# The passage from the long convolution into the MLP: copies and turns in halves, two tiles normalised on VectorE, ten fillers, and a new list order

## Chip, core and metric

One core of a Trainium2 chip runs the whole program. TensorE (PE in the rows; PEld is its weight load) multiplies, VectorE (DVE), ScalarE (ACT) and GpSimd (POOL) work on elements, SyncE (SP) issues most transfers. The metric is the device time of one execution in microseconds, the median of three runs. The profile is one more execution, read on its own clock: 0 is the start of the span.

## The reference, cut to what matters

An adaptive-LayerNorm block on 2048 rows of 640 columns in bf16. First half: normalise, scale and shift by a modulation, then a gated long convolution over the rows (a length-4096 Fourier product, done here as matrix products), times q, added to x. Second half: normalise again, scale and shift, then a gated MLP (gMLP) whose gate mixes rows by a 2048 x 2048 matrix.

```python
h = _layernorm(x, axis=-1) * (1 + ca) + sa
x = x + ga * _A_ref(h, A_k, A_v, A_shift_k, A_ssm_k, A_ssm_D)     # y = irfft(rfft(kv) * rfft(ssm_k)), q * y
h = _layernorm(x, axis=-1) * (1 + cb) + sb
z = _gelu(einsum('bsd,df->bsf', h, w_in))                         # 864 columns z1, 864 columns z2
g = einsum('ts,bsf->btf', w_sp, _layernorm(z2)) + b_sp
x = x + gb * einsum('bsf,fd->bsd', z1 * g, w_out)
```

The second normalisation needs all 640 columns of a row, so the MLP can begin only when the last 128 columns of the convolution are done. That place is the passage.

## The kernel before

The convolution runs in five units u = 0 to 4 of 128 columns. Per unit there are eight stages st: a forward product into `pu` (matrices M), a product with the filter's spectrum on VectorE (`prod`, L495: `Tf` or `T`), in half the stages a sum on GpSimd or VectorE (`csum`, L509: `W`), an inverse product into `pz` (matrices G) and a copy `zc` of 128 x 512 into `Z`, on ScalarE (L278, helper `copy`). Then the rows have to be turned: units 0 to 3 by a DMA transpose of `Z` into `ZT` and products `y` with `Ebd` (`y_mult`, VectorE multiply `ym` at L770), unit 4 on TensorE (`last_stage_pe`): four blocks of eight 128 x 128 transposes (`zfl`, L831) into `pu`/`pz`, four copies `zk` of 128 x 1024 into two `X` buffers, then products `yl` of 128 x 16 for each of four row groups g (512 rows each), a multiplication `yml` (L856), the addition to x `res` (L808) and statistics `ln2` (L814).

`norm_piece` and `flip_piece` make the MLP's input of group 0 in two pieces of two row tiles n: `ag2` gathers statistics (L943), GpSimd makes 1/sqrt in two instructions (`rstd_from_var`, L218 and L219), VectorE makes `nmr2` (L947), any of three engines normalises (`zx`, L957/L959/L961), TensorE transposes (`hfl`, L972), VectorE and ScalarE scale and shift (`hmod`, L985/L983). `z_group` then multiplies: a `zz` is five matmuls of 128 x 432 into `pu`/`pz`, sixteen `zz` a group, 64 in all, each followed by a gelu on ScalarE (L1034). Groups 1 to 3 are turned by a DMA transpose from SyncE (L1003) and scaled by five `hmod2` (L1011/L1009). After that come the mixing products (L1126) and the projections (L1335, L1348).

What sets the order: `Plan.op` records every piece of work with the engines that may run it and what it reads and writes; the string `ORDER` lists engine and number of each, and `run` emits them in that order. Each engine works through its own list strictly in order, waiting where an operand is not there yet. Buffers come from `SLOTS`. `FILLS` gives the matmuls (128 x 512, `ident` times `ident`) in each of the `fill` entries, whose result nothing reads; in this kernel three of them run near the start and one stands ahead of the first `zz`.

Of the kernel before, what the change touches and what calls it, by code (L numbers as in the profile page):

```python
# [15 lines left out]
P = 128  # L16
# [8 lines left out]
NU = 5  # L25
# [12 lines left out]
FILLS = (4, 2, 2, 2, )  # L38
# [9 lines left out]
G5 D18 A1 S83 G0 G110 S2 P7 S23 G109 G6 D13 A4 D14 G25 A16 D15 D111 P1041 D10 S26 D112 P8 A38 D17 D113 A11 G89 D130  # L48
A115 D136 P1044 S24 P153 S84 S91 A154 P156 P39 D131 P41 A158 A133 A132 S27 P1043 G90 D118 G134 D40 A137 D119 S3 A114
P45 A155 A157 D124 P159 D125 S531 D135 P162 G96 A121 A120 D42 A160 G122 P43 D19 S532 A161 A127 G116 P235 D46 A163 G117  # L50
A126 A164 D44 D128 P141 G129 D20 P85 P179 A21 G22 A236 P173 D142 G143 A180 D86 A174 P241 P9 A242 D535 G123 S28 D29 P87
P181 D88 P184 D183 A182 P239 A186 P167 P177 S30 G47 A12 P147 D539 A168 P165 A178 A240 A166 D536 A537 P144 D148 S31 P175
A176 G139 D540 D145 P237 P187 A185 A541 D189 P48 P54 S534 P171 D188 D49 D55 P190 A172 D192 P50 P52 D51 A191 G56 D53
P193 P219 P92 P150 S573 A238 S97 A538 D194 P225 S533 D93 D220 G32 G146 G195 P57 G149 G196 A151 P94 P169 D226 G152 P259
A542 A170 P203 P209 D58 A260 P61 P197 G65 D95 A550 P265 D204 D221 D62 G205 P574 D210 P229 G222 D230 G206 A198 G102 D543
A266 P59 P223 P261 A551 P247 S576 P213 D60 A575 A262 P207 A248 P63 S33 A224 D214 P199 A552 D200 P263 D546 P227 A264
P249 G544 A250 P243 A244 D64 P577 G74 D34 P309 G231 D578 G215 A208 A310 P98 P255 A256 P257 P211 P267 D545 S579 D547
G557 G232 P311 G216 A258 S35 D99 D548 A553 G561 A228 D268 A312 P100 D549 P66 D101 P251 P277 A252 D554 A212 P233 D278
A234 P313 P245 P201 D269 P580 A314 G558 G562 D67 D581 P315 S103 G270 G555 D556 P253 A202 A246 P283 P271 A316 P591 D559
# [98 lines left out]
def kernel(  # L158
# [80 lines left out]
    with ExitStack() as pctx:  # L239
# [578 lines left out]
        def last_stage_pe(u):  # L818
# [3 lines left out]
            for b, qb in enumerate(range(0, NQ, QB)):  # L822
# [640 lines left out]
```

## Time and profile before

| | |
|---|---|
| runs (us) | 305.56, 306.22, 306.85, median 306.22 |
| span of the profiled execution | 303.8 us |
| TensorE busy | 293.1 us (96%) |
| VectorE, GpSimd, ScalarE busy | 86%, 61%, 54% |
| TensorE's granted clock | full, but for a stretch from 127 to 133.8 us |

No time but the span is known for the profiled execution. The runs' median is 2.4 us above it; what lies around the span is taken as unchanged. Busy time of TensorE is close to the span, but pipelined matmuls count as busy also while they are spaced widely, so the passage has to be read in time order.

### The profile page before, as it was taken

The numbers are of one execution on the slowest core, as the hardware profiler recorded it, in microseconds if no ns is written. First come the engines' busy times: TensorE is split into PE (matmuls) and PEld (weight loads), VectorE is DVE, ScalarE is ACT, GpSimd is POOL, SyncE is SP. The second block draws the span as 40 slices with busy tenths as digits, with TensorE's granted clock in tenths as the row PEclk, the third lists the DMA queues.
The fourth block names the chain that finished last, engine by engine and source line by source line (L and its number), as shares of the span: only waits on it lengthen the run. The fifth ranks groups of instructions, "written<-read, shape, count | busy, mean of one in ns | idle before, by whom it ended". The sixth has DMA issues, their size and how long they took to land.

```text
span 303.8 us, 7152 instructions
## 1 busy us (share of the span) xinstructions
PE 293.1 (96%) x2827; PEld 207.0 (68%) x2827; DVE 260.4 (86%) x527; ACT 164.0 (54%) x299; POOL 186.8 (61%) x213
## 2 busy tenths in 40 slices
PE   6899999999999999799999999999999999999996
PEld 2788999999989988645555555555555555665664
DVE  8899999999989999989595988988678798886794
ACT  5989999998888865446665779500111102111110
POOL 5463788839769997577537342099531863476771
PEclk9999999999999999869999999999999999999999
DMA  7999869792397978005997900057654446452433
GB/s 143 270 242 271 194 177 282 134 223 39 77 186 163 287 122 276 2 2 105 157 234 154 197 0 4 0 117 150 132 133 90 102 112 141 102 84 73 91 83 121
DMA packets 117155, 41.57 MB, mean 137 GB/s; under 512 B 102557, under 2 KB 117122, under 8 KB 117122
## 3 DMA queue, kind: packets, MB, share of 16 engines
q1 hardware_dynamic: 116968, 41.08, 62.0%
q8 instruction: 22, 0.36, 0.5%
q14 instruction: 11, 0.09, 0.1%
q10 hardware_dynamic: 154, 0.05, 0.1%
HBM read 16.60 MB, written 2.63 MB: 63 GB/s over the span
## 4 chain that ended last, share of the span: by engine, by line
PE 80%; DVE 8%; SPq 5%; DMA 3%; issue 2%; POOL 1%; ACT 0%; DVEq 0%; POOLq 0%
PE ps L1126 23%; PE pu L275 19%; PE pz L275 17%; PE po L1335 5%; PE sm L275 5%; PE s L275 4%; SPq L570 3%; DVE Tf L495 3%; PE po L1348 3%; DMA ZT<-in_A_v_dram 3%; PE pz L1126 2%; PE pu L1126 1%; DVE Z L616 1%; SPq L585 1%; DVE ot L1394 1%
## 5 line engine op out<-in xcount | busy, mean ns | idle before, releaser
L275 PEld LDWEIGHTS <-Z 128*128 128x128 bf16 x320 | 32.0, 100 | 28.8 <-issue 3.0
L275 PE MATMUL pu<-X,M 128*128 128x128 bf16 (+1 forms) x480 | 45.6, 237 | 0.9 <-DVE Tf L495 0.7
L509 POOL TENSOR_TENSOR W<-Tf 128x256 bf16<-128x256 f32 x42 | 30.7, 745 | 15.0 <-DVE Tf L495 9.0
L275 PEld LDWEIGHTS <-M 128*128 128x128 bf16 x480 | 36.7, 98 | 4.2 <-issue 1.6
L1126 PEld LDWEIGHTS <-S 128*128 128x128 bf16 x256 | 25.0, 98 | 20.8
L275 PE MATMUL pu<-big,Z 128*128 128x432 bf16 x160 | 34.6, 360 | 0.0
L278 ACT CAST X<-s 128x1024 bf16<-128x1024 f32 x32 | 32.7, 1021 | 3.3 <-PE s L275 3.2
L275 PE MATMUL pz<-big,Z 128*128 128x432 bf16 x160 | 33.0, 349 | 0.0
L495 DVE TENSOR_TENSOR Tf<-pu,KH 128x1024 f32<-128x1024 f32 x25 | 30.3, 1215 | 1.2 <-ACT Z L278 0.5
L1132 ACT COPY m<-ps 128x432 f32<-128x432 f32 x7 | 3.6, 521 | 49.8 <-PE ps L1126 41.0
L1126 PEld LDWEIGHTS <-wT 128*128 128x128 bf16 x192 | 18.8, 98 | 15.3
L278 ACT CAST Z<-pz 128x512 bf16<-128x512 f32 x40 | 23.5, 596 | 4.9 <-PE pz L275 4.7
L275 PEld LDWEIGHTS <-G 128*128 128x128 bf16 x330 | 24.6, 98 | 1.8 <-issue 0.4
L278 ACT CAST KH<-pu 128x512 bf16<-128x512 f32 x40 | 23.1, 592 | 3.8 <-PE pu L275 3.4
L1126 PE MATMUL ps<-X,wT 128*128 128x432 bf16 x112 | 22.7, 346 | 0.0
L1126 PE MATMUL ps<-X,S 128*128 128x432 bf16 x112 | 22.6, 346 | 0.0
L1040 DVE BATCH_NORM_STATS2 stz<-X 128x6 f32<-128x432 bf16 x32 | 18.1, 588 | 5.0 <-ACT X L1034 4.9
L1126 PE MATMUL ps<-T,S 128*128 128x432 bf16 x112 | 22.2, 346 | 0.0
L275 PE MATMUL sm<-dg,big 128*128 128x128 bf16 x320 | 20.7, 219 | 1.1 <-DVE Z L616 1.0
L275 PEld LDWEIGHTS <-big 128*128 128x128 bf16 x320 | 18.9, 98 | 2.0 <-issue 1.6
L495 DVE TENSOR_TENSOR T<-pu,KH 128x1024 bf16<-128x1024 f32 x15 | 18.2, 1215 | 1.9 <-PE pu L275 1.8
L275 PEld LDWEIGHTS <-X 128*128 128x128 bf16 x288 | 17.8, 98 | 2.2 <-POOL X L433 0.7
(223 smaller groups left out, 666.7 us busy)
## 6 DMA issues: line engine op xcount, KB each, us to landing
wm<-in_w_mod_dram SPq DMA_DIRECT2D x6, 800.0 KB, 4.9
xt<-in_A_q_dram SPq DMA_DIRECT2D x4, 640.0 KB, 5.6
out_dram<-ot SPq DMA_DIRECT2D x15, 160.0 KB, 1.9
big<-in_B_w_in_dram SPq DMA_DIRECT2D x2, 1080.0 KB, 7.8
X<-in_A_ssm_k_dram SPq DMA_DIRECT2D x4, 512.0 KB, 6.2
ZT<-in_A_v_dram SPq DMA_DIRECT2D x1, 1024.0 KB, 7.6
big<-in_A_v_dram SPq DMA_DIRECT2D x1, 1024.0 KB, 7.8
w_o<-in_B_w_out_dram SPq DMA_DIRECT2D x6, 160.0 KB, 3.5
```

Source lines behind the costliest of these rows:

```text
L275: nc.tensor.matmul(o, lhsT=w, rhs=x, start=start, stop=stop)
L278: (e.copy if e is nc.scalar else e.tensor_copy)(dst, src)
L495: e.tensor_tensor(T_[:], (tl[pu] if src is None else tl[src])[:, :, :, None, :].to_broadcast(shape), tl[KH][:, :, None, :, :].to_broadcast ...
L509: e.tensor_tensor(tl[W][:, :, o, :], T_[:, :, 0, o, :], T_[:, :, 1, 1 - o, :], op=ALU.add if o else ALU.subtract)
L570: e.dma_start_transpose(k_of(u)[:, KPAD + h * m:KPAD + (h + 1) * m], A_k[0, h * m:(h + 1) * m, u * DU:(u + 1) * DU])
L585: e.dma_start(v_of(0, ns.start, NT // n) if u0 == 0 else tl[name][:], v_nat[:, ns, ds])
L616: e.tensor_tensor(dst, tl[ps][:].rearrange("p n (c g) -> p n c g", g=8), v_of(u, i * SCH, SCH).rearrange("p n (c g) -> p n c g", g=8), op= ...
L1040: op("D", "stz", lambda e, i=i, n=n, fc=fc: e.bn_stats(out=stz[:, n, fc, :], in_=tl[z2][:, i, fc * FC:(fc + 1) * FC]), r=[(z2, (i, fc))], ...
L1126: nc.tensor.matmul(ps[:, :FC], lhsT=lhs[:, s_, :], rhs=rhs(s_), start=(s_ == 0 and not more), stop=(s_ == HT - 1), skip_group_check=more)
L1132: e.copy(part[p, m][:], part[p, BANK[m]][:, :FC])
L1335: nc.tensor.matmul(ps[:, :HS], lhsT=w(k), rhs=x(k), start=start and k == 0, stop=stop and k == n - 1, skip_group_check=True)
L1348: e.matmul(po[t, i][:, :hi - lo], lhsT=uTs[t][:fsz[ft], ft, :], rhs=T["w_o"][:fsz[ft], ft, lo:hi], start=(ft == 0), stop=(ft == NFT - 1))
```

## The change

Six edits, all but the last in code that serves the passage, and a new order.

1. The copy `zc` of unit 4's stage 4 (`LAST`) is cut in two 128 x 256 halves, which two engines can share.
2. The four turns `zfl` and copies `zk` of unit 4 become eight each (four transposes; 128 x 512), and group 0's products `yl` come in eight parts instead of four, each needing one half copy.
3. For the first piece of group 0 (`quick`) the constant EPS is added on VectorE right behind the last `ag2`, GpSimd does only the power, `nmr2` is left out, and `zx` must run on VectorE.
4. `hfl` goes by row tile: five transposes for one tile, then five for the other, instead of six and four that need both.
5. `res` of unit 4 may run on GpSimd for groups 1 to 3.
6. Six more `fill` entries of one matmul each (`FILLS`).

```diff
+LAST = 4
-FILLS = (4, 2, 2, 2, )
+FILLS = (4, 2, 2, 2, 1, 1, 1, 1, 1, 1)
...
-P45 A155 A157 D124 P159 D125 S531 D135 P162 G96 A121 A120 D42 A160 G122 P43 D19 S532 A161 A127 G116 P235 D46 A163 G117
+P45 A155 A157 D124 P159 D125 S532 D135 P162 G96 A121 A120 D42 A160 G122 P43 D19 S533 A161 A127 G116 P235 D46 A163 G117
...
+    def rstd_from_var(dst, var_ap, eps=True):
+        if eps:
+            nc.gpsimd.tensor_scalar(dst, var_ap, EPS, 1.0, op0=ALU.add, op1=ALU.mult)
+            var_ap = dst
+        nc.gpsimd.tensor_tensor(dst, var_ap, mhalf[:, 0:dst.shape[1]], op=ALU.pow)
...
+            parts = KP if u == NU - 1 and st == LAST else 1
+            for h in range(parts):
+                k0, k1 = h * KP // parts, (h + 1) * KP // parts
...
-            op("GD" if u < NU - 1 else "D", "res", lambda e: e.tensor_tensor(sl, sl, gl, op=ALU.add),
+            op("GD" if u < NU - 1 or g else "D", "res", lambda e: e.tensor_tensor(sl, sl, gl, op=ALU.add),
...
+                for h in range(2):
+                    def flips(e, qb=qb, pt=pt, tag=tag, h=h):
+                        if h == 0:
+                            new(pt, tag, [P, QB, P])
+                        for i in range(h * QB // 2, (h + 1) * QB // 2):
+                            e.transpose(tl[pt][:, i, :], tl[Z][:, qb + i, :, :].rearrange("p j c -> p (j c)"), ident[:])
...
-                tag, k = "pz" if g % 2 else "sm", 4 if g == 0 else 1
+                tag, k = "pz" if g % 2 else "sm", 8 if g == 0 else 1
...
+            quick, gs = g == 0 and p == 0, slice(ns[0], ns[-1] + 1)
...
+                    if quick and n == ns[-1]:
+                        e.tensor_scalar(mv2[:, gs, 1], mv2[:, gs, 1], EPS, None, op0=ALU.add)
...
+            op("G", "rstd2", lambda e: rstd_from_var(rstd2[:, gs], mv2[:, gs, 1], not quick), r=[("mv2", n) for n in ns], w=[("rs2", (g, p))], n=len(ns))
+            if not quick:
+                op("D", "nmr2", lambda e: e.scalar_tensor_tensor(nmr2[:, gs], mv2[:, gs, 0], -1.0, rstd2[:, gs], op0=ALU.mult, op1=ALU.mult),
...
+                op("D" if quick else "DAG", "zx", norm, r=[("mv2", n), ("rs2", (g, p))] + ([] if quick else [("nm2", (g, p))]) + [("xt", (u, n)) for u in range(NU)] + ([] if first else [(xn2, "new")]),
...
+            for i in range(k):
+                def flips(e, i=i):
+                    for dts, tag in halves:
```

Up to the last inverse products of unit 4 the list is the same but for the numbers. From there on it is new, on all engines.

VectorE in the passage, from its half of the last sum `W` on (`sm` are the products `y`, `X` the turned unit 4, `gh` what is added to x, `mv2` mean and variance). Before:

```order
L509 TENSOR_TENSOR W_2663<-Tf_2622 128x2x128
L770 TENSOR_TENSOR gh_95<-gh_95,sm_2641 128x16x8x4
L770 TENSOR_TENSOR gh_95<-gh_95,sm_2668 128x16x8x4
L814 BN_STATS st2_72<-xt_68 128x6
L770 TENSOR_TENSOR gh_95<-gh_95,sm_2688 128x16x8x4
L278 COPY X_2716<-pu_2698 128x1024
L770 TENSOR_TENSOR gh_95<-gh_95,sm_2720 128x16x8x4
L278 COPY X_2716<-pz_2730 128x1024
L808 TENSOR_TENSOR xt_68<-xt_68,gh_95 128x4x128
L814 BN_STATS st2_72<-xt_68 128x6 x2
L856 TENSOR_TENSOR gh_95<-gh_95,sm_2776 128x2x128
```

Now:

```order
L515 TENSOR_TENSOR W_2649<-Tf_2647 128x2x128
L823 BN_STATS st2_72<-xt_68 128x6
L779 TENSOR_TENSOR gh_95<-gh_95,sm_2655 128x16x8x4
L779 TENSOR_TENSOR gh_95<-gh_95,sm_2665 128x16x8x4
L284 CAST Z_2536<-pz_2683 128x32x8
L779 TENSOR_TENSOR gh_95<-gh_95,sm_2692 128x16x8x4
L779 TENSOR_TENSOR gh_95<-gh_95,sm_2704 128x16x8x4
L284 COPY X_2742<-pu_2729 128x512
L284 COPY X_2746<-pz_2719 128x512 x2
L284 COPY X_2746<-pu_2724 128x512
L823 BN_STATS st2_72<-xt_68 128x6
L870 TENSOR_TENSOR gh_95<-gh_95,sm_2757 128x2x128
```

VectorE now also takes one half of the last `zc` behind two multiplications and four half `zk` behind two more; the addition of 128 x 512 (L808) and one of the two statistics have left the place ahead of the first `yml` (L856, now L870).

GpSimd over the same stretch. Before:

```order
L753 TENSOR_TENSOR gh_95<-gh_95,gsa_bf_102 128x4x128
L509 TENSOR_TENSOR W_2566<-Tf_2563 128x2x128 x2
L509 TENSOR_TENSOR W_2610<-Tf_2607 128x2x128 x2
L509 TENSOR_TENSOR W_2663<-Tf_2622 128x2x128
L808 TENSOR_TENSOR xt_68<-xt_68,gh_95 128x4x128
L753 TENSOR_TENSOR gh_95<-gh_95,gsa_bf_102 128x4x128 x2
L218 TENSOR_SCALAR rstd2_83<-mv2_82 128x2
L219 TENSOR_TENSOR rstd2_83<-rstd2_83,mhalf_76 128x2
L959 TENSOR_SCALAR Z_2935<-xt_68,rstd2_83,nmr2_84 128x640
```

Now:

```order
L762 TENSOR_TENSOR gh_95<-gh_95,gsa_bf_102 128x4x128
L515 TENSOR_TENSOR W_2551<-Tf_2549 128x2x128 x2
L817 TENSOR_TENSOR xt_68<-xt_68,gh_95 128x4x128
L515 TENSOR_TENSOR W_2620<-Tf_2578 128x2x128 x2
L515 TENSOR_TENSOR W_2649<-Tf_2647 128x2x128
L817 TENSOR_TENSOR xt_68<-xt_68,gh_95 128x4x128
L762 TENSOR_TENSOR gh_95<-gh_95,gsa_bf_102 128x4x128
L817 TENSOR_TENSOR xt_68<-xt_68,gh_95 128x4x128
L225 TENSOR_TENSOR rstd2_83<-mv2_82,mhalf_76 128x2
L817 TENSOR_TENSOR xt_68<-xt_68,gh_95 128x4x128 x2
```

One addition to x now stands between two pairs of sums, another (taken from VectorE) ahead of the power, and no normalisation follows the power.

VectorE where row group 1 is normalised, further down the list (`nmr2` of 128 x 4 is group 1's, `Z` first its normalised and then its turned tile). Before:

```order
L947 SCALAR_TENSOR_TENSOR nmr2_84<-mv2_82,rstd2_83 128x4
L814 BN_STATS st2_72<-xt_68 128x6
L961 TENSOR_SCALAR Z_3049<-xt_68,mv2_82,rstd2_83 128x640 x2
L814 BN_STATS st2_72<-xt_68 128x6 x4
L1040 BN_STATS stz_85<-X1_2980 128x6
L808 TENSOR_TENSOR xt_68<-xt_68,gh_95 128x4x128
```

Now:

```order
L965 SCALAR_TENSOR_TENSOR nmr2_84<-mv2_82,rstd2_83 128x4
L979 TENSOR_SCALAR Z_3070<-xt_68,mv2_82,rstd2_83 128x640 x3
L870 TENSOR_TENSOR gh_95<-gh_95,sm_2939 128x4x128
L817 TENSOR_TENSOR xt_68<-xt_68,gh_95 128x4x128 x2
L823 BN_STATS st2_72<-xt_68 128x6 x3
L817 TENSOR_TENSOR xt_68<-xt_68,gh_95 128x4x128
L823 BN_STATS st2_72<-xt_68 128x6 x5
L1033 TENSOR_SCALAR Z_3075<-Z_3075,cb1_col_70,sb_col_71 128x4x128 x5
```

VectorE normalises three of group 1's four tiles instead of two, and all five `hmod2` are its own; before, it had two of them, GpSimd two and ScalarE one.

On TensorE the new list has, from the last forward product on: two fillers, the inverse products with the `y` products between them, one filler, eight `zfl`, eight parts of `yl`, three fillers, `yl` of group 1, the last modulation product, a filler of two, `yl` of group 3, `hfl` of two tiles, `yl` of group 2, and the first `zz` with no filler ahead of it. SyncE's list keeps its order up to the last weight load; the transfers of `gb` now stand ahead of group 1's turn.

## Rows read from the trace of the kernel before

**Rows 1.** The page: span, and the granted TensorE clock in 40 slices, in tenths.

```profile
span 303.8 us, 7152 instructions
PEclk9999999999999999869999999999999999999999
```

**Rows 2.** Waits of TensorE from 128 us to the end: total, times, longest.

```profile
PE s L275 <- DVE Z L985: 0.8, 1, 0.8
PE po L1335 <- DVE ot L1394: 0.2, 1, 0.2
```

**Rows 3.** Stretches: length, busy PE, PEld, DVE, ACT, POOL; clock; DMA share, GB/s.

```profile
126.00:128.00 2.00, 1.10 (x10) 0.84 (x10) 1.96 (x7) 0.67 (x2) 2.00 (x3) 0.75 0.00 0
132.00:134.00 2.00, 2.00 (x7) 0.86 (x6) 2.00 (x7) 0.91 (x2) 1.94 (x2) 0.54 0.00 0
```

**Rows 4.** GpSimd in time order: start, length, what, [idle before, releaser].

```profile
114.51 1.41 POOL L509 TENSOR_TENSOR W<-Tf 128x256 bf16<-128x256 f32 x2 [0.51 <-DVE Tf L495]
116.77 0.98 POOL L509 TENSOR_TENSOR W<-Tf 128x256 bf16<-128x256 f32 x1 [0.85 <-DVE Tf L495]
117.70 1.16 POOL L808 TENSOR_TENSOR xt<-xt,gh 128x512 bf16<-128x512 bf16 x1
```

**Rows 5.** The chain that ended last, through the passage: start, length, what.

```profile
118.44 0.59 ACT Z L278
119.08 0.64 PE pu L831 x8
119.74 0.69 DVE X L278
120.43 0.68 DVE gh L770
...
122.14 0.75 DVE st L814 x2
122.89 0.33 DVE gh L856
...
124.06 0.28 DVE mv L943 x2
...
124.43 0.19 POOL rstd L218
...
124.70 0.82 POOL rstd L219
...
125.88 0.88 POOL Z L959
...
126.81 0.69 PE s L972 x6
...
127.58 1.06 DVE Z L985 x3
...
136.02 0.91 PE pu L275 x5
```

**Rows 6.** TensorE in time order, from the fillers to group 0's second piece.

```profile
128.69 1.03 PE L275 MATMUL s<-ident 128*128 128x512 bf16 x2 [0.78 <-DVE Z L985]
129.51 3.81 PE L275 MATMUL pu<-big,Z 128*128 128x432 bf16 x10
...
135.30 0.50 PE L972 MATMUL s<-ident,Z 128*128 128x128 bf16 x6
135.63 0.39 PE L972 MATMUL sm<-ident,Z 128*128 128x128 bf16 x4
```

**Rows 7.** Group 1's input in time order: normalise, turn, scale.

```profile
137.40 0.79 DVE L961 TENSOR_SCALAR Z<-xt,mv,rstd 128x640 bf16<-128x640 bf16 x2
137.53 1.32 POOL L959 TENSOR_SCALAR Z<-xt,rstd,nmr 128x640 bf16<-128x640 bf16 x1 [1.64 <-ACT Z L983]
...
138.88 3.00 SPq L1003 DMA_TRANSPOSE Z<-Z  x1
...
143.86 0.43 DVE L1011 TENSOR_SCALAR Z<-Z,cb_col,sb_col 128x512 bf16<-128x512 bf16 x1
...
144.41 0.58 DVE L1011 TENSOR_SCALAR Z<-Z,cb_col,sb_col 128x512 bf16<-128x512 bf16 x1
...
145.11 0.81 ACT L1009 ACTIVATE Z<-Z,sb_col,cb_col 128x512 bf16<-128x512 bf16 x1
```

More of the change, by code (lines that the diff above doesn't have):

```diff
@@ L108 @@
[L108 to L111 removed]
+G5 D18 A1 S83 G0 G110 S2 P7 S23 G109 G6 D13 A4 D14 G25 A16 D15 D111 P1053 D10 S26 D112 P8 A38 D17 D113 A11 G89 D130
@@ L112 @@
+D1460 S1455 S1461 A1458
 """
@@ L823, in last_stage_pe @@
                 pt, ZT, low = "pt%d_%d" % (u, qb), "ZT%d_%d" % (u, b // 2), b % 2 == 0
-                ZTs.append((ZT, b % 2))
+                ZTs += [(ZT, b % 2 * 2 + h) for h in range(2)]
                 tag = "pz" if b % 2 else "pu"
-                def flips(e, qb=qb, pt=pt, tag=tag):
-                    p_ = new(pt, tag, [P, QB, P])
-                    for i in range(QB):
-                        e.transpose(p_[:, i, :], tl[Z][:, qb + i, :, :].rearrange("p j c -> p (j c)"), ident[:])
@@ L961, in norm @@
                         e.tensor_scalar(dst, xt[:, n, :], mv2[:, n, 0:1], rstd2[:, n:n + 1], op0=ALU.subtract, op1=ALU.mult)
-                op("DAG", "zx", norm, r=[("mv2", n), ("rs2", (g, p)), ("nm2", (g, p))] + [("xt", (u, n)) for u in range(NU)] + ([] if first else [(xn2, "new")]),
+                op("D" if quick else "DAG", "zx", norm, r=[("mv2", n), ("rs2", (g, p))] + ([] if quick else [("nm2", (g, p))]) + [("xt", (u, n)) for u in range(NU)] + ([] if first else [(xn2, "new")]),
                    w=[(xn2, n % TB)] + ([(xn2, "new")] if first else []), new=[(xn2, "Z")] if first else [])
@@ L966, in flip_piece @@
             k, i0 = len(ns), ns[0] % TB
[L967 to L974 removed]
+            halves = ((range(0, 3), "s1"), (range(3, ND), "sm"))
+            for i in range(k):
+                def flips(e, i=i):
+                    for dts, tag in halves:
+                        pt = "ft%d_%d" % (p, dts[0])
+                        if i == 0:
+                            new(pt, tag, [P, len(dts), k, P])
+                        for j, dt in enumerate(dts):
+                            e.transpose(tl[pt][:, j, i, :], tl[xn2][:, i0 + i, dt * P:(dt + 1) * P], ident[:])
+                pts = [("ft%d_%d" % (p, dts[0]), tag) for dts, tag in halves]
+                op("P", "hfl", flips, r=["ident", (xn2, i0 + i)] + [(pt, "new") for pt, _ in pts] * (i > 0),
+                   w=[(pt, i) for pt, _ in pts] + [(pt, "new") for pt, _ in pts] * (i == 0), new=[] if i else pts, n=ND)
             for dt in range(ND):
```

173 lines of the change are left out of this document (82 added, 91 removed).

## Prediction

> **What bounds the kernel now.** I read the page first, for the span and the clock line: TensorE's clock is granted in full but for two slices in the middle [rows 1]. Then TensorE's waits: behind 128 us it waits 0.8 us once and 0.2 us once [rows 2], so from the first `zz` to the end its own work sets the time, and whatever brings that work forward by 1 us is worth 1 us, unless a later input is then late. Ahead of 128 us lies the passage. The chain of waits shows a single file of small steps there: the last copy `zc` starts at 118.44, turns from 119.08, the first `yml` at 122.89, statistics done at 124.34, GpSimd's 1/sqrt until 125.52, a normalisation until 126.76, transposes, and `hmod` until 128.64 [rows 5]. Then two fillers hold TensorE until 129.51, when the first `zz` starts [rows 6]. The reader should see two losses. From the last `zc` to the first `zz` it takes 11 us in which TensorE has only thin work; and the clock falls to half in this stretch (0.75 on average over 126 to 128, still 0.54 over 132 to 134 [rows 3]), so that the first twenty matmuls of `zz` take 129.51 to 135.30, 5.79 us [rows 6], where five take 0.91 at full clock [rows 5].
>
> **The change, part by part.** Times are on the clock of the profiled span of 303.8 us [rows 1]; 2.4 us more lie between it and the runs' median of 306.22, and I leave those as they are.
>
> (a) Up to the last `zc`: nothing won. The last inverse product waits for GpSimd's half of the last `W`, done at 117.75 [rows 4]. An addition of 1.16 is put ahead of the pair of sums that starts at 114.51. GpSimd stood idle 0.51 before that pair and 0.85 before the last sum [rows 4]; the addition can start at 114.00, the pair moves to 115.16 and ends at 116.57, 0.2 before the last sum is released at 116.77. That idle time hides it; with the cover gone everything behind moves by the excess. Two single fillers (half of 0.82 for two at half clock [rows 6], so 0.2 each at full) stand where TensorE waits for these sums. The cut of `zc`: 256 columns cost between half of the 0.59 for 512 and all of it [rows 5]; I take 0.4. ScalarE's half ends earlier, but VectorE's stands behind a statistic (0.38, half of 0.75) and two multiplications of 0.68 [rows 5], which with its own sum fill 116.8 to about 118.7. So `Z` is whole at 119.1 against 119.03: between 0.3 gained and 0.2 lost, I take 0.
>
> (b) Turns and copies in halves: 0.6 earlier. A transpose takes 0.055 (six in the 0.33 from 135.30 to 135.63 [rows 6]), 32 in a row 1.8, so they are done at 120.9 and hide behind the copies. ScalarE copies four halves of 512 columns at 0.59 each (the `zc` row, same width [rows 5]) from 119.4: 121.8. VectorE has two more multiplications of 0.68, until 120.5, then four halves, each between half and all of 0.69 [rows 5]; at 0.38, near the half as the price is mostly per column, 122.0. The last part of `yl` is four matmuls behind it. The addition that stood ahead of `yml` is now GpSimd's: 1.16 from about 120.5, done 121.7, hidden by the copies. One statistic still stands ahead of `yml`. So `yml` starts at 122.3 instead of 122.89 (122.0 to 122.8).
>
> (c) Statistics: 0.1 earlier. Before, 122.89 to 124.34 is 1.45 [rows 5]. Now one statistic more (0.38) and the addition of EPS, a tiny instruction priced as an aggregation (0.14, half of 0.28 [rows 5]): 1.97, done at 124.27.
>
> (d) Normalising: 0.5 earlier. GpSimd keeps the power, 0.82, and loses the 0.19 ahead of it (0.27 from start to start [rows 5]): done at 125.15 instead of 125.52. The stretch of 0.36 from 125.52 to 125.88 with `nmr2` in it goes. But VectorE is not free at once: two `yml` (0.33, and at most 0.68 for the wide one) and an addition bring it to 125.4. Two normalisations there take 0.79 [rows 7]: 126.2, against 126.76. The first tile's five transposes run meanwhile, the other five follow in 0.28 at full clock: `hmod` starts at 126.6 instead of 127.58 and ends 1.06 later [rows 5], at 127.65. No filler stands behind it, which returns the 0.82 of 128.69 to 129.51 [rows 6]. First `zz`: 127.75, 1.76 earlier.
>
> Here a rule of the Trainium skill speaks against the change. The row first: when two of VectorE's normalisations ran beside one of GpSimd's, VectorE's pair took 0.79, and GpSimd's took 1.32 instead of 0.88 [rows 5, 7]; GpSimd paid. "SBUF — State Buffer", section "SBUF: two separate sides", says that the two engines share a port pair held by whichever starts first for its whole instruction, while the other blocks fully. In the new list GpSimd starts an addition of 1.16 right behind the power. By the row the sum stands; by the rule the normalisation waits until 126.3, 0.9 later. It is a rival below.
>
> (e) The clock: 2.1 us. Four `zz` at full clock are about 3.65 (4 x 0.91) instead of 5.79, if the clock holds. Before the fall TensorE stood still from the last `yl` to 126.81, 1.4 us, behind thin products. Now fillers (three of 0.2, then a pair) lie among the `yl`, which are spread up to the first `zz`; I find no gap above 0.4 us between 119 and 128. All fillers stand where TensorE would wait for VectorE; if one is late it costs 0.2.
>
> (f) What is late next: group 1's input, about 0.45 us given back. With (d) and (e) TensorE wants it after sixteen `zz` and the second piece's transposes: 127.75 + 16 x 0.91 + 0.56 = 142.9; before, the same count from 135.30 gives 146.8. It was ready at 145.92 [rows 7], with 0.9 to spare, so it must come 3 us sooner. VectorE's list from 127.65 to the normalisation holds about 11 statistics (0.3 on average), 6 aggregations (0.14), two wide multiplications (0.68), two additions (0.35), three `hmod` (1.06) and two small ones: some 7.6 us, 135.2. Three normalisations of 0.4 give 136.4. Turn and landing took 138.88 to 143.86, 4.98 [rows 7]: 141.4. Five `hmod2` on VectorE, 0.43 to 0.58 each but overlapped [rows 7], take 1.8 to 2.6: 143.2 to 144.0; with less waiting between VectorE's steps it is 142.7. Stall between 0 and 1.0, taken as 0.45. Later groups have had more to spare. Behind the MLP's first half the list is nearly the old one and TensorE-bound, so the gain stays.
>
> Sum: 1.76 + 2.14 - 0.45 = 3.45. The span becomes 300.35, the median 306.22 - 3.45 = 302.8.
>
> **Rivals.**
> *The clock falls anyway.* The new passage still has about 5 us of thin products, and the fillers are small. For it: the fall before came after just such work. Against: the 1.4 us standstill is gone. Half clock lasted until near 134 [rows 3]; if it ends there again, only the earlier start at half speed, 0.9 us, is won: 305.3. If it falls and rises 2 us sooner, 304.4. I take 305.0.
> *Inputs of groups 1 and 2 come too late.* Group 2's tiles are three in file on GpSimd, 0.88 to 1.32 each [rows 5, 7]. Stalls of 1.5 to 2.5 instead of 0.45: 303.9 to 304.9.
> *The shared port.* The normalisations wait for GpSimd's addition: 0.9 later, 303.7.
> *VectorE becomes the bound, and it is slower than before.* It takes over three normalisations and three `hmod2`, and 20 us of its list lie end to end from 122 to 143. If its steps take their full length in place of the overlapped one (0.58 against 0.43 for the same `hmod2` [rows 7]), a quarter more, group 1 is 5 us later and GpSimd's three tiles of 1.32 hold group 2 a further 1.3: 306.2 - 3.9 + 5 + 1.3 = 308.6. It decides from the point where group 1 is ready after 148.3. Against it: VectorE was busy 1.96 of 2 us in 126 to 128 [rows 3] and kept up.
> *The change does not do what it says.* Halves save nothing, being bound by the slower engine, and the clock falls as before: 306.2.
>
> **How the numbers follow.** Forecast 302.8 (302.0 to 303.6 with the bounds of (b) and (f)): 0.50. Clock falls: 0.20. Late groups: 0.11. Shared port: 0.06. Nothing won: 0.06. Slower: 0.07. The runs spread by 0.6 to either side. From 301.6 to 305.6 the range leaves out some 0.03 below and 0.16 above. A measurement of this kernel can tell 0.5%, 1.5 us, from no change: below 304.7 is faster, above 307.75 slower. Faster: 0.50 + 0.06 + most of the late groups, 0.09, + the milder third of the clock's rival, 0.06 = 0.71. Slower 0.07, the rest 0.22.
>
> **What would show it.** In the changed kernel's clock line no slice below 9 between 118 and 136 us (e); the first `yml` near 122.3, the power done near 125.2, two normalisations on VectorE ending near 126.2, the first `zz` near 127.8 and 0.91 for five from the start (b to e); a wait of TensorE for `hmod2` of group 1 under 1 us (f). The forecast is wrong if the clock's granted share is 0.5 under the first `zz`, if that `zz` starts after 129, if TensorE waits more than 1.5 us in the 64 `zz`, or if the normalisations start only when GpSimd's addition ends.

## The result, and the profile after

The changed kernel is slower: 309.52 us (median of 4 runs, 309.08 to 310.43) against 306.12 (4 runs of before on the same chip, 305.56 to 306.85), a ratio of 1.0119, interval 1.0085 to 1.0152. The forecast was 302.8 with a range to 305.6. The profiled execution of after took 309.87 us, with a span of 308.1; that of before 305.56 and 303.8 [rows 1]. So 1.8 us lie around the span in either; the 2.4 of the forecast held another 0.6, because the profiled run of before was the lowest of its runs.

The spans differ by 4.3 us, but 1.1 of it lies ahead of the change. VectorE's first forward product already starts 1.08 later in the profile of after (28.82 instead of 27.74), where the two lists are the same, and its last one ends 1.08 later too. The two rows of the last one, of before and then of after (start, length, what):

```profile
115.42 1.21 DVE L495 TENSOR_TENSOR Tf<-pu,KH 128x1024 f32<-128x1024 f32 x1
```

```profile
116.50 1.21 DVE L501 TENSOR_TENSOR Tf<-pu,KH 128x1024 f32<-128x1024 f32 x1
```

I take that as chance: VectorE's first forward product started between 27.67 and 29.25 us in the profiles of this study, and at the latest, 29.25, in a kernel (e10 below) whose list up to there is that of before. So I measure from the end of the last forward product, 116.63 in before and 117.71 in after. From there on after is 3.2 longer, which agrees with the medians' 3.4. Step by step (the forecast's times are put on the same zero):

| from | to | before | forecast | after |
|---|---|---|---|---|
| last forward product | first turn `zfl` | 2.45 | 2.45 | 2.91 |
| first turn | first `yml` | 3.73 | 3.2 | 3.32 |
| first `yml` | power on GpSimd done | 2.71 | 2.85 | 2.73 |
| power done | second normalisation done | 1.24 | 1.05 | **2.83** |
| normalisation | first `zz` | 2.76 | 1.55 | 1.64 |
| first `zz` | fifth `zz` | 6.34 | 4.2 | 4.84 |
| zero | fifth `zz` | 19.23 | 15.3 | 18.27 |
| zero | group 1's input ready | 29.29 | 26.7 | **31.37** |
| zero | last `zz` done | 74.14 | | 75.88 |
| zero | first projection | 95.88 | | **99.06** |
| zero | end | 187.2 | | 190.4 |

The clock line of after still has a slice below full; the one of before is in [rows 1]:

```profile
span 308.1 us, 7166 instructions
PEclk9999999999999999899999999999999999999999
```

TensorE's waits from 125 to 225 us in after (total, times, longest); before had one of 0.8 there, behind group 0's `hmod` [rows 2]:

```profile
PE s L993 <- DVE Z L979: 1.3, 1, 1.3
PE pz L1148 <- ACT m L1156: 0.9, 1, 0.9
PE pz L281 <- DVE Z L1033: 0.8, 1, 0.8
PE pu L281 <- DVE Z L1033: 0.6, 1, 0.6
PE pz L281 <- ACT X L1056: 0.3, 1, 0.3
PE pz L1148 <- DVE c L1177: 0.2, 1, 0.2
```

All but the 0.3 for a gelu (L1056) are waits for VectorE, or for ScalarE behind it: for the normalised tile (L979), for the scaled input of groups 1 and 2 (L1033), and at the mixing products (L1148), where ScalarE had itself waited 1.54 for `nmrz`, which VectorE makes from the last 1/sqrt of z.

**The cause, in rows.** GpSimd and then VectorE, around the first normalisation in after (start, length, what, [idle before, releaser]):

```profile
125.97 0.71 POOL L225 TENSOR_TENSOR rstd<-mv,mhalf 128x2 f32<-128x2 f32 x1 [3.38 <-DVE mv L961]
126.65 2.31 POOL L817 TENSOR_TENSOR xt<-xt,gh 128x512 bf16<-128x512 bf16 x2
```

```profile
124.40 0.29 DVE L817 TENSOR_TENSOR xt<-xt,gh 128x256 bf16<-128x256 bf16 x1
...
126.72 1.23 DVE L817 TENSOR_TENSOR xt<-xt,gh 128x256 bf16<-128x256 bf16 x1
127.88 1.62 DVE L979 TENSOR_SCALAR Z<-xt,mv,rstd 128x640 bf16<-128x640 bf16 x2
```

The same addition of 128 x 256 takes 0.29 at 124.40 and 1.23 at 126.72. Its start is 0.07 behind the start of GpSimd's addition, its end (127.95) 0.15 behind the end of it (127.8, half of 2.31 after 126.65). The next VectorE instruction then starts behind GpSimd's second addition and ends 0.2 behind that: the first of the two normalisations takes 1.27 (1.62 from 127.88 less 0.35 for the second). Two VectorE instructions that need 0.7 together have lasted 2.5.

Before, GpSimd ran two such additions at the same place, and they cost VectorE little, because most of what it did beside them read TensorE's results out of PSUM (`pz`, `s`). GpSimd, then VectorE, in before:

```profile
126.72 2.26 POOL L808 TENSOR_TENSOR xt<-xt,gh 128x512 bf16<-128x512 bf16 x2
```

```profile
126.95 0.63 DVE L856 TENSOR_TENSOR gh<-gh,pz 128x512 bf16<-128x512 bf16 x1
127.58 1.05 DVE L985 TENSOR_SCALAR Z<-s,cb_col,sb_col 128x256 bf16<-128x256 bf16 x3
```

The same multiplication takes 0.62 at 129.66, with no such addition beside it, and the same three scalings 1.05 in after, at 130.28, where GpSimd stands idle. So it is not the additions that are new, but what VectorE does beside them.

The holding recurs where GpSimd has just started and VectorE works between SBUF tiles. Group 1's `nmr` of 128 x 4, 0.15 in before, behind an addition that GpSimd started 0.06 earlier, and the normalisation after it; VectorE, then GpSimd, then SyncE's turn:

```profile
138.45 1.11 DVE L965 SCALAR_TENSOR_TENSOR nmr<-mv,rstd 128x4 f32<-128x4 f32 x1 [0.20 <-POOL rstd L225]
139.49 2.06 DVE L979 TENSOR_SCALAR Z<-xt,mv,rstd 128x640 bf16<-128x640 bf16 x3
```

```profile
138.39 2.26 POOL L817 TENSOR_TENSOR xt<-xt,gh 128x512 bf16<-128x512 bf16 x2
```

```profile
141.64 3.06 SPq L1025 DMA_TRANSPOSE Z<-Z  x1
```

and near the end of the MLP's first half, where GpSimd multiplies `w_o` (VectorE, then GpSimd):

```profile
179.56 0.93 DVE L1071 SCALAR_TENSOR_TENSOR nmrz<-mvz,rstdz 128x4 f32<-128x4 f32 x1
...
187.07 1.52 DVE L1079 TENSOR_SCALAR X<-X,mvz,rstdz 128x864 bf16<-128x864 bf16 x1
```

```profile
179.06 2.75 POOL L1225 TENSOR_TENSOR w_o<-w_o,gb_bf 128x640 bf16<-128x640 bf16 x2
...
186.96 1.39 POOL L1225 TENSOR_TENSOR w_o<-w_o,gb_bf 128x640 bf16<-128x640 bf16 x1
...
192.11 1.70 POOL L225 TENSOR_TENSOR rstdz<-rstdz,mhalf 128x4 f32<-128x4 f32 x1
```

The last of these rows is the last 1/sqrt of z, done at 193.81. Taking from each stretched VectorE instruction what the same one costs elsewhere: 0.94 + 0.83 in the passage, 0.96 + 0.92 at group 1, 0.50 + 0.57 at two `hmod2` of group 2, 0.78 + 1.04 here. That is 6.5 us of VectorE's time between 126 and 190; in before the same count gives 2.8 (an `nmrz` at 161.43 of 1.35 instead of 0.15, and six of 0.2 to 0.4).

The Trainium skill has this in "SBUF — State Buffer", section "SBUF: two separate sides": a VectorE instruction in a 2-port mode or with two SBUF inputs and a GpSimd instruction lock the shared port pair for whole instructions, and the one that starts first has it. These rows agree: in three of the places GpSimd is ahead by 0.06 to 0.11 us, and VectorE pays about 1.

### The profile page after: what moved, and what is told of

The parts are those of the page before. It is cut to its first block, busy times and chain, and to the rows that moved or that the text cites. A ratio compares the mean times of both kernels' runs of the same rounds, so it can differ in the third digit from the quotient of the medians.

```text
span 308.1 us, 7166 instructions
## 1 busy us (share of the span) xinstructions
PE 293.9 (95%) x2833; PEld 206.6 (67%) x2833; DVE 267.1 (87%) x536; ACT 163.7 (53%) x299; POOL 183.5 (60%) x208
## 3 DMA queue, kind: packets, MB, share of 16 engines
HBM read 16.60 MB, written 2.63 MB: 62 GB/s over the span
## 4 chain that ended last, share of the span: by engine, by line
PE 64%; DVE 20%; SPq 5%; DMA 4%; issue 3%; POOL 1%; ACT 1%; DVEq 0%; ACTq 0%
PE ps L1148 23%; PE pu L281 13%; PE pz L281 10%; PE po L1357 5%; PE sm L281 5%; PE s L281 3%; SPq L579 3%; DVE stz L1062 3%; DVE Tf L501 3%; DMA ZT<-in_A_v_dram 2%; PE po L1370 2%; DMA Z<-Z 2%; DVE X L1079 1%; DVE st L823 1%; DVE T L1133 1%
## 5 line engine op out<-in xcount | busy, mean ns | idle before, releaser
L281 PEld LDWEIGHTS <-Z 128*128 128x128 bf16 x320 | 31.1, 98 | 30.2 <-DVE Z L1033 3.1
L1148 PEld LDWEIGHTS <-S 128*128 128x128 bf16 x256 | 25.0, 98 | 21.9 <-issue 1.2
L281 PE MATMUL pu<-big,Z 128*128 128x432 bf16 x160 | 33.5, 351 | 0.6 <-DVE Z L1033 0.6
L1148 PEld LDWEIGHTS <-wT 128*128 128x128 bf16 x192 | 18.8, 98 | 15.6 <-issue 0.4
L284 ACT CAST Z<-pz 128x512 bf16<-128x512 f32 (+1 forms) x40 | 23.2, 590 | 5.5 <-PE pz L281 5.0
L1148 PE MATMUL ps<-X,wT 128*128 128x432 bf16 x112 | 22.7, 346 | 0.0
L1148 PE MATMUL ps<-X,S 128*128 128x432 bf16 x112 | 22.6, 346 | 0.0
L1148 PE MATMUL ps<-T,S 128*128 128x432 bf16 x112 | 22.2, 346 | 0.0
```

The source lines that it names most:

```text
L281: nc.tensor.matmul(o, lhsT=w, rhs=x, start=start, stop=stop)
L284: (e.copy if e is nc.scalar else e.tensor_copy)(dst, src)
L1148: nc.tensor.matmul(ps[:, :FC], lhsT=lhs[:, s_, :], rhs=rhs(s_), start=(s_ == 0 and not more), stop=(s_ == HT - 1), skip_group_check=more)
```

## The experiments

Two theories at first. **Sharing**: VectorE is held behind GpSimd's instructions, and the time goes where the new list lets GpSimd start first. **Clock and passage**: the halves and the six fillers cost more than they give. An addition on GpSimd can be put behind a VectorE instruction by letting it first read one element of that instruction's result into a spare tile (`held`); that computes nothing of the output.

**e1, e2: hold GpSimd's additions back.** In e1 two additions stand behind the two quick normalisations; e2 does the same at group 1 too.

```diff
-D753 D758 G677 S589 ... D783 D784 P597 G759 P771
+D753 D758 S589 ... D783 D784 G677 G759 P597 P771
...
+                behind = {(2, 1): ('xn2_0', 1)}.get((u, g))
+                if behind:
+                    e.tensor_copy(held[:], tl[behind[0]][:, behind[1], 0:1])
                 e.tensor_tensor(sl, sl, gl, op=ALU.add)
```

and in e2

```diff
+                behind = {(2, 1): ('xn2_0', 1), (0, 2): ('xn2_1', 1)}.get((u, g))
```

> The changed kernel with one thing more: behind the first power, GpSimd reads one element of the second normalised tile before its two additions of 128x512, so these start when both normalisations on VectorE are done and not at the same time as VectorE's addition and first normalisation. Theory A (the two engines exclude each other: whoever starts first keeps the other waiting for its whole instruction): VectorE's addition of 128x256 goes back from 1.23 to about 0.3 and the first normalisation from 1.27 to about 0.43, the first zz starts 1.7 us earlier against the last forward product, and the kernel falls from 309.5 to about 307.8. Theory B (VectorE has too much work, whatever GpSimd does): the two instructions stay at 1.2, GpSimd's additions end 2 us later, and the time is 309.5 to 310.5.

> As the kernel that holds the two additions behind the first power, and the same once more for row group 1: GpSimd's two additions behind group 1's power wait for a normalised tile of that group. Theory A: nmr2 of group 1 goes from 1.11 to 0.16 and its first normalisation from 1.35 to 0.43, group 1's input is ready 1.8 us earlier against the first zz, TensorE's wait of 0.6 for hmod2 of group 1 goes, and the time is 0.6 to 1.2 below the kernel with one hold: 306.6 to 307.2. Theory B: VectorE is late anyway, the time is as with one hold or up to 1 us above it, since the additions that later statistics need come later.

e1: 307.79 (306.85 to 308.83, 5 runs), 1.0065 of before (1.0041 to 1.0089). VectorE in e1, where 126.72 and 127.88 stood in after:

```profile
126.00 0.28 DVE L822 TENSOR_TENSOR xt<-xt,gh 128x256 bf16<-128x256 bf16 x1
126.20 0.80 DVE L985 TENSOR_SCALAR Z<-xt,mv,rstd 128x640 bf16<-128x640 bf16 x2
```

```profile
127.06 0.19 POOL L821 COPY held<-Z 128x1 bf16<-128x1 bf16 x1 [1.11 <-DVE Z L985]
127.20 2.26 POOL L822 TENSOR_TENSOR xt<-xt,gh 128x512 bf16<-128x512 bf16 x2
```

The same instructions take 0.28 and 0.80 instead of 1.23 and 1.62: the second normalisation ends 1.8 earlier, the whole of the misfit in the table. The first `zz` comes only 0.9 earlier, not the 1.7 that I expected: the profiled run is the slowest of e1's five, and its clock was at half from 126 to 132. In e2, whose list is the same up to there, the profiled run kept the full clock, and the first `zz` comes 2.0 earlier than in after. Group 1's input is ready only 0.24 earlier in e1 than in after, because `nmr` and the normalisation are held again there (1.12 and 2.06, as in after) and because the turn took 6.29 to land instead of 5.61; TensorE then waits 1.2 for it. With the second place mended, VectorE in e2:

```profile
136.57 0.16 DVE L971 SCALAR_TENSOR_TENSOR nmr<-mv,rstd 128x4 f32<-128x4 f32 x1 [0.21 <-POOL rstd L226]
136.65 1.15 DVE L985 TENSOR_SCALAR Z<-xt,mv,rstd 128x640 bf16<-128x640 bf16 x3
```

Group 1's input is ready at 27.46, 3.9 earlier than in after, and the kernel takes 305.93 (304.98 to 308.04, 10 runs), 1.0018 (0.9993 to 1.0044), below the range expected: all of after's loss is gone. Nothing was taken out of either engine's work. VectorE is still held for 4.7 us by the count above (6.5 in after), but elsewhere. Behind group 1's normalisations, VectorE and then GpSimd in e2:

```profile
138.32 2.42 DVE L822 TENSOR_TENSOR xt<-xt,gh 128x512 bf16<-128x512 bf16 x2
```

```profile
138.00 3.74 POOL L822 TENSOR_TENSOR xt<-xt,gh 128x512 bf16<-128x512 bf16 x3
```

Two additions of 0.4 last 2.42, but no wait of TensorE hangs on them. So it matters less how long VectorE is held than which of its instructions are.

Part of the gain came with the clock. Seven of e2's ten runs had a mean granted clock of 0.999 or 1.0, where after's four had 0.989 to 0.994; its three at 0.989 took 307.70 to 308.04, still above before. So some 2 of the 3.6 us came only where the clock stayed full, and what kept it up is not separated from the holds.

**e5: share less on the whole stretch.** e1, and three additions and two normalisations of group 3 given from GpSimd to VectorE, one sum of mixing weights put further back on VectorE's list, and GpSimd's three multiplications of `w_o` put together and held behind a normalisation.

```diff
-G620 ... G621 ... G766 ... G996 ... G995
+D620 ... D621 ... D766 ... D996 D995
-D1079 ... D1080 ... G1074 ... G1075 ... G1073
+G1074 G1075 G1073 D1079 D1080
...
+                if ft == 3:
+                    e.tensor_copy(held[:], tl["xn2_3"][:, 2, 0:1])
```

> The kernel with one hold, and every other place where GpSimd's long instructions ran beside VectorE's additions, normalisations and scalings is taken apart: three additions to x of groups 2 and 3 and two normalisations of group 3 go from GpSimd to VectorE (about 0.35 and 0.43 each there), GpSimd's three multiplications of w_o run in the stretch where VectorE only takes statistics, and the first sum S on VectorE, which waits 1.6 for a transfer while statistics stand ready behind it, moves behind these statistics. Theory A (the exclusion, and not VectorE's amount of work, makes it late): no VectorE instruction over 0.9 between the last forward product and the last z statistics except the wide ones, the last 1/sqrt of z 3 to 5 us earlier than with two holds (which had 72.0 after the last forward product), TensorE's wait of 1.3 for m goes, and the time is 303.6 to 304.4. Theory B (VectorE's own work, now more of it, is the bound): the last 1/sqrt of z stays within 1 us and the time is 305.4 to 306.5.

304.77 (303.31 to 306.62, 10 runs), 0.9961 (0.9937 to 0.9984): faster than before. VectorE has more work than in after, and the last 1/sqrt of z is done 70.57 behind zero instead of 76.09. VectorE is held for 1.0 us in all by the count above, once, at a normalisation of z beside GpSimd's fourth multiplication of `w_o`. The time lies between the two ranges that I had given, nearer to that of exclusion: against e2 the last 1/sqrt came 1.4 earlier and not 3 to 5, and a wait of 0.4 for m was left. GpSimd's multiplications of `w_o` (the first row) now lie beside statistics, which VectorE runs at 0.53 each, as it does alone:

```profile
159.14 4.11 POOL L1233 TENSOR_TENSOR w_o<-w_o,gb_bf 128x640 bf16<-128x640 bf16 x3
```

```profile
161.09 3.16 DVE L1068 BATCH_NORM_STATS2 stz<-X 128x6 f32<-128x432 bf16 x6 [1.40 <-ACT X L1062]
```

**e6: the late part alone**, on after: the `w_o` multiplications put together and that one sum moved, nothing held.

```diff
-D1079 ... D1080 S1065 G995 ... G1074 ... G1075 ... G1073
+D1079 D1080 S1065 G995 G1074 G1075 G1073
```

> The changed kernel with only the late part mended: GpSimd's three multiplications of w_o directly behind its last normalisation, and VectorE's first sum S behind the statistics that stand ready. If VectorE's lateness at the end of the MLP's first half is a loss of its own: nmrz goes from 0.93 to 0.15, a normalisation of z from 1.52 to 0.45, the last 1/sqrt of z comes 2 to 3 us earlier, TensorE's 0.9 to 1.2 for m go, and the time is 307.9 to 308.5. If it only follows from the late inputs of groups 1 to 3: 309.2 to 309.8.

309.42 (308.12 to 309.82, 4 runs), 1.0102 (1.0073 to 1.0131), no gain. The collision only moved: `nmrz` is short, but four `hmod2` of group 2, 2.42 in after, now take 3.50 beside the same multiplications, and TensorE's wait for them went from 0.8 to 1.8.

```profile
161.00 3.50 DVE L1033 TENSOR_SCALAR Z<-Z,cb_col,sb_col 128x512 bf16<-128x512 bf16 x4 [0.20 <-DMA Z<-Z]
```

```profile
162.94 4.17 POOL L1225 TENSOR_TENSOR w_o<-w_o,gb_bf 128x640 bf16<-128x640 bf16 x3
```

So this run doesn't price the late part by itself; it shows that a place without a hold is a place for the next collision.

**e3, e7, e8: the six new fillers**, taken from after, taken from e5, and put into before (one ahead of the first `yl` of group 2, three behind it, two behind the first `hfl`).

```diff
-FILLS = (4, 2, 2, 2, 1, 1, 1, 1, 1, 1)
+FILLS = (4, 2, 2, 2, 0, 0, 0, 0, 0, 0)
```

and in e8

```diff
-FILLS = (4, 2, 2, 2, )
+FILLS = (4, 2, 2, 2, 1, 1, 1, 1, 1, 1)
...
-P744 ... P751 ... P774
+P744 P1045 ... P751 P1046 P1047 P1048 ... P774 P1049 P1050
```

> The changed kernel without its six new fillers (the entries stand in the list and issue nothing; the filler of two stays). If the fillers hold the clock up: the stretch at half clock, 3.4 us in the changed kernel, becomes about 6.8 as in the kernel before, the first zz run 1.5 us longer, and the time is about 311. If they do nothing for it, or the clock falls for another reason: the stretch stays within 0.5 us of 3.4, and the time is 309.3 to 309.6.

> The kernel with less sharing, without the six new fillers. If the fillers hold the clock up: the mean granted clock is 0.989 in most runs, as in the kernel before, and the time 1.5 to 2.2 above the kernel with less sharing (two holds: 305.7 in runs at full clock, 307.9 in runs at 0.989). If the shorter standstill ahead of the first zz does it alone: clock at or above 0.999 in most runs and the time within 0.4 of the kernel with less sharing.

> The kernel before with only the six fillers of one matmul, put where TensorE waits in its passage: one behind the yl of group 2, three behind that of group 3, two behind the first transposes. If standing still is what lets the clock fall: mean clock near 1.0, the first four zz take 3.65 instead of 5.79, group 1's input is then up to 1.2 late, and the time is 304.6 to 305.3. If the clock falls anyway: 305.6 to 306.5. Its list up to the passage is that of the kernel before, so its first forward product also shows whether the 1.1 us by which the changed kernel's profile is late there is chance: then it lies anywhere from 27.7 to 28.8 us.

e3: 309.35 (308.87 to 309.73, 4 runs), 1.0115; as after. The clock stays at half longer, as expected of fillers that hold it up (its fifth `zz` starts 0.74 later), and yet the time is not the 311 that went with that, since group 1's input is waited for in either case. e7: 304.54 (304.03 to 304.57, 4 runs), 0.9946 (0.9927 to 0.9964); the time is as in e5, but the mean clock is 0.989 to 0.994 in its four runs, where seven of e5's ten had 0.999 or 1.0. e8: 308.0 (307.55 to 308.35, 4 runs), 1.0062 (1.0042 to 1.0082): in before the fillers are a loss, outside both of the ranges expected. TensorE in e8:

```profile
125.70 1.87 PE L275 MATMUL s<-ident 128*128 128x512 bf16 x3
...
129.62 2.32 PE L275 MATMUL s<-ident 128*128 128x512 bf16 x4 [0.78 <-DVE Z L985]
131.74 3.80 PE L275 MATMUL pu<-big,Z 128*128 128x432 bf16 x10
```

The clock was at half already when all but the first of them ran: 0.6 each instead of the 0.2 that I had priced, and the clock was half in every 2 us from 126 to 134. The first `zz` comes 2.0 later than in before.

**e4: the last `zc` in one piece**, on ScalarE as before.

```diff
-                k0, k1 = h * KP // parts, (h + 1) * KP // parts
+                k0, k1 = (0, KP) if not h else (0, 0)
```

> The changed kernel with the copy zc of the last stage in one piece of 128x512 on ScalarE; VectorE's half is left out of its list. Theory C (the two halves run one behind the other, ScalarE's starting 0.03 after VectorE's end, so the cut costs): Z is whole 0.2 us earlier, the turns start 0.2 us earlier against the last forward product, VectorE's multiplications come 0.4 earlier, and the first yml 0.2 to 0.4 earlier; the time is 309.1 to 309.4. Theory D (the cut saves what it was priced at): Z is whole 0.2 to 0.3 later, time 309.5 to 309.8.

The two halves in after, VectorE's and ScalarE's, of one and the same `pz`:

```profile
119.75 0.42 DVE L284 CAST Z<-pz 128x256 bf16<-128x256 f32 x1
```

```profile
120.20 0.37 ACT L284 CAST Z<-pz 128x256 bf16<-128x256 f32 x1 [0.39 <-DVE Z L284]
```

They don't run side by side: ScalarE's starts 0.03 behind the end of VectorE's, which it waits for. "PSUM — Partial Sum Buffer", section "PSUM bank collisions raise a hardware error" of the Trainium skill says that two engines may not touch one bank at a time and that the compiler's scheduler adds a dependency between two that would, reads too; the wait in this row agrees with that, though no run separates it from a wait for the tile `Z`, which both halves write. In one piece, the copy and the first `yml` come 0.28 earlier, as far as expected, but the kernel took 310.78 (309.33 to 312.72, 4 runs), 1.017 (1.0126 to 1.0214), above both of the ranges expected. In its profiled run, the slowest of the four, group 2's turn landed 6.75 after its issue (at most 5.72 in after, 156.56 to 162.28), and the clock fell a second time:

```profile
PEclk9999999999999999799997999999999999999999
```

Why that transfer was slower isn't shown, nor whether it was in the other three runs; alone, this edit could not be priced.

**e9, e11, e12: together.** e9 is e7 with the last `zc` in one piece and the fourth multiplication of `w_o` beside the other three. e11 puts the six fillers back; e12 takes the old filler of two ahead of the first product of the MLP away. e10 does the latter to before. The edits of e9 (beside that of e4), e10, e11 and e12 in this order:

```diff
-G1075 G1073 D1079 ... G1071
+G1075 G1073 G1071 D1079
...
-FILLS = (4, 2, 2, 2, )
+FILLS = (4, 0, 2, 2, )
...
-FILLS = (4, 2, 2, 2, 0, 0, 0, 0, 0, 0)
+FILLS = (4, 2, 2, 2, 1, 1, 1, 1, 1, 1)
...
-FILLS = (4, 2, 2, 2, 0, 0, 0, 0, 0, 0)
+FILLS = (4, 0, 2, 2, 0, 0, 0, 0, 0, 0)
```

> What helped, together: less sharing, no new fillers, the last copy zc in one piece on ScalarE, and GpSimd's fourth multiplication of w_o with the other three (it held a normalisation of z on VectorE for 1.53 instead of 0.45). Theory A (exclusion and the serial halves are what cost): the turns start 0.2 to 0.3 earlier after the last forward product (2.6), the last 1/sqrt of z about 1 us earlier than without the fillers (71.3), the wait of 0.4 for m goes, and the time is 303.7 to 304.2. Rival (the end of the MLP's first half is bound by something else): within 0.3 of the kernel without the fillers, 304.3 to 304.8.

> The kernel before with only the filler of two matmuls ahead of its first zz left out. If that filler is plain cost (0.82 in the profile of before, and no filler held the clock in the other runs): the first zz starts 0.8 earlier after the last forward product (12.1 instead of 12.9), group 1's input still comes in time or 0.1 late, and the time is 0.6 to 0.9 under that of before, 305.2 to 305.6. If it shortens the stretch at half clock: that stretch becomes longer by up to 3.4 us and the time is the same or up to 1 us longer.

> e9 (the moves and the holds together, without the six new fillers: 303.17) with the six new fillers put back. If the new fillers bring time once the passage is short (the profile at full clock through the passage, as in most runs of e2 and e5), 302.5 to 302.9. If they bring only the clock and no time, as the equal medians of e5 (304.77) and e7 (304.54) say, 303.0 to 303.6, whatever the clock.

> e9 without the filler of two matmuls that stands ahead of the first forward product of the MLP, the one that the kernel before has too. If that filler is plain cost in the short passage as it was in e10 (first product 1.3 earlier, median 1.4 to 1.8 lower than before), 302.3 to 302.9, with the first product 0.5 to 1.0 earlier than in e9. If its cost is already hidden there by the wait for the first normalised tile, 303.0 to 303.6.

| | us (runs) | ratio to before | first `zz` | fifth `zz` |
|---|---|---|---|---|
| e9 | 303.17, 301.92 to 304.80 (6) | 0.9913, 0.9883 to 0.9942 | 11.18 | 17.17 |
| e10 | 304.28, 303.63 to 305.79 (10) | 0.9957, 0.9939 to 0.9974 | 11.57 | 17.75 |
| e11 | 303.54, 302.38 to 303.88 (6) | 0.9914, 0.9893 to 0.9935 | 11.11 | 15.36 |
| e12 | 303.98, 303.22 to 304.41 (6) | 0.9927, 0.9906 to 0.9949 | 11.18 | 16.02 |

e9 and e11 are the best: 0.9% ahead of before, 2% ahead of after. In e9's profile no VectorE instruction between 125 and 191 us takes 0.15 more than the same one elsewhere, and its median is below both of the ranges expected. In e10 the filler of two was plain cost, 1.3 at the first `zz` and 1.4 in the median, more than the 0.6 to 0.9 expected. In e12 it was not, and the median lies above both of the ranges expected, 302.3 to 302.9 and 303.0 to 303.6: the first `zz` does not move, since TensorE waits 0.6 for the normalised tile in either kernel. In e11 the fillers do what they were put in for. TensorE's first ten matmuls of `zz` in e9 and then in e11, and e11's clock line:

```profile
128.37 3.76 PE L282 MATMUL pu<-big,Z 128*128 128x432 bf16 x10
```

```profile
127.68 2.03 PE L282 MATMUL pu<-big,Z 128*128 128x432 bf16 x10
```

```profile
span 300.6 us, 7165 instructions
PEclk9999999999999999999999999999999999999999
```

Five of e11's six runs had a granted clock of 0.999 or 1.0 over the span, one of e9's six. The medians are the same all the same. That is the second of the two expectations for e11, clock and no time; but in e11's profile the last `zz` ends 1.1 earlier behind zero than in e9's, and inside one kernel the clock does tell: e2's seven runs at 0.999 or 1.0 took 304.98 to 306.88, its three at 0.989 307.70 to 308.04. Where e11 gives this back was not found; its profiled run, 302.38, was the lowest of its six, and no other was traced.

## Why the prediction was wrong, step by step

**(d) is the step that failed.** It took from [rows 5, 7] that GpSimd pays when both engines normalise (1.32 instead of 0.88), and put VectorE's two normalisations at 0.79, as if they overlapped freely with GpSimd's additions. In that row VectorE had started first, at 137.40 against 137.53. The row never showed what happens when GpSimd is first. In the new list its additions stand right behind the power: in the passage VectorE came to its own addition 0.07 behind them, from a multiplication, and at group 1, where the end of the power releases both engines, GpSimd was ahead by 0.06. From the power to the second normalisation it took 2.83 instead of 1.05. e1 only puts the two additions behind the normalisations, and the 1.8 come back.

**The rival of the shared port** had the mechanism, and was mis-sized. I priced it once, at 0.9, for one normalisation. It cost 0.94 + 0.83 in the passage alone, since the addition ahead of the normalisations waits too, and it comes back at group 1, at group 2 and where z is normalised. e2 shows that with two of these places mended the loss against before is gone, in part by way of the clock. The price in the text made 303.7 and the chance was put at 0.06; the kernel took 309.5. The condition that I had written for being wrong, normalisations that start only when GpSimd's addition ends, is what the trace shows.

**(a)** "Z is whole at 119.1": it was 0.46 later than in before. I had let the two halves run side by side; they ran one behind the other. Not all of the 0.46 is theirs: the turn comes 0.40 late with the halves and without the six fillers (e3, 2.85 behind zero), 0.18 late with the fillers and the copy whole (e4, 2.63), and not late with neither (e9, 2.45). The fillers ahead of the turns, put at nothing, were not free.

**(b)** Halves gave 0.41 between the first turn and the first `yml`, forecast 0.6. (a) took all of it. **(c)** was close: with the power, 2.73, forecast 2.85, before 2.71. The last part of (d), from the normalisation to the first `zz` without a filler, came out near the forecast of 1.55 partly by luck: 1.64 with the clock at half, 1.39 at full clock in e2.

**(e)** "3.65 at full clock": the first four `zz`, up to the second piece's turns, took 4.28 (131.15 to 135.43) where before took 5.79 [rows 6], so 1.5 of the 2.1 came. The clock still fell while TensorE stood still for the normalised tile. TensorE in after, and stretches of it (length, busy PE, PEld, DVE, ACT, POOL; clock; DMA share, GB/s):

```profile
129.20 0.50 PE L993 MATMUL s<-ident,Z 128*128 128x128 bf16 x3 [1.31 <-DVE Z L979]
...
131.15 2.62 PE L281 MATMUL pu<-big,Z 128*128 128x432 bf16 x10
```

```profile
126.00:128.00 2.00, 1.90 (x52) 1.31 (x48) 2.00 (x4) 0.42 (x2) 2.00 (x3) 1.00 0.04 8
128.00:130.00 2.00, 0.80 (x8) 0.80 (x9) 2.00 (x4) 0.00 (x0) 0.96 (x1) 0.76 0.09 31
130.00:132.00 2.00, 2.00 (x40) 1.55 (x38) 1.72 (x8) 1.02 (x2) 0.00 (x0) 0.50 0.17 51
132.00:134.00 2.00, 2.00 (x12) 0.97 (x10) 1.85 (x7) 0.73 (x2) 1.25 (x3) 0.88 0.00 0
```

The gap of 1.31 is the held normalisation again. At 126 to 128 the clock was full, where before had 0.75 [rows 3].

**(f)** "a stall of 0.45": at the fifth `zz` after was still 0.96 ahead of before, as the table says. Group 1's input then came 2.1 later than in before instead of 2.6 earlier, and the lead was lost there. Not because of the five scalings, which I had at 1.8 to 2.6:

```profile
147.38 1.71 DVE L1033 TENSOR_SCALAR Z<-Z,cb_col,sb_col 128x512 bf16<-128x512 bf16 x5 [1.74 <-DMA Z<-Z]
```

but because the turn was issued 1.68 later behind zero than in before (23.93, right behind the two held instructions, which lost 0.96 + 0.92; before 22.25 [rows 7]) and the first scaling started 5.74 behind the issue (5.61 of it to landing), not 4.98. The scalings gave 0.35 back (1.71 for 2.06 from 143.86 to 145.92 [rows 7]). "Behind the MLP's first half the gain stays" was wrong as well: between the last `zz` and the first projection 1.4 more were lost, to the waits of 0.9 and 0.2 in the list above, behind the last 1/sqrt of z, which was 4.2 late.

**VectorE becomes the bound** was the rival nearest in time, 308.6. TensorE did wait for VectorE, and VectorE's steps were longer, but not for the reason given, its amount of work or steps that no longer overlap: e5 gives it more work and is 4.7 us faster than after.

## What to carry to other kernels

When a stretch hands work between VectorE and GpSimd, ask of every pair that runs together which of the two starts first. Where both work between SBUF tiles, as these additions and normalisations did, the second one waits to the end of the first one's instruction, so a short instruction on the path pays for a long one off it. A row that shows the other engine paying tells only who was first there. Hold GpSimd's other work behind the VectorE instruction that the path needs, at every such place on the path at once: e1's gain at one place was mostly lost at the next, and in e6 the collision moved.

## What the runs showed of the hardware

- Not every VectorE instruction is held. Additions, multiplications and normalisations between SBUF tiles were (an `nmr` of 128 x 4 took 1.11 instead of 0.15; a multiplication of 128 x 512 at 128.54 in before 0.72 instead of 0.41). Statistics were not (0.53 each beside GpSimd's multiplications, e5), nor were a multiplication and scalings with an operand in PSUM (0.63 and 1.05 beside additions in before).
- Two engines that read halves of one `pz` tile took turns, with 0.03 us between them.
- A filler matmul of 128 x 512 cost 0.6 us at half clock, and fillers put among thin work in before did not keep the clock up (e8), while in the shorter passage of e2, e5 and e11 it stayed full in most runs. A standstill of TensorE is not what it takes for the fall: in the profiles of e8 and e9 the clock was at half from 125.3 and 125.2 on, and from 118 us up to there TensorE never stood still for more than 0.44 us. What makes the difference is not settled.
- The start of the program varies by 1.6 us between profiles of kernels whose lists are the same up to there (first forward product at 27.67 to 29.25), as much as many a change is worth. These are the two ends, in e11 and e10:

```profile
27.67 1.22 DVE L502 TENSOR_TENSOR Tf<-pu,KH 128x1024 f32<-128x1024 f32 x1
```

```profile
29.25 1.22 DVE L495 TENSOR_TENSOR Tf<-pu,KH 128x1024 f32<-128x1024 f32 x1
```
